# Packed 64-row TensorE products and ScalarE-issued stores in an FFT convolution gated with a GLU

## The chip, the cores and the metric

The kernel runs on one core of a Trainium2 chip. The metric is device time in microseconds (us) of one execution; lower is better. A core has five engines that each work through an instruction list of their own in order: PE (TensorE, the matmuls), DVE (VectorE), ACT (ScalarE), POOL (GpSimd) and SP (SyncE). In this kernel SP computes nothing; it issues the DMA transfers between on-chip memory (SBUF) and device memory (DRAM). Matmul results land in PSUM, in banks of 128 partitions by 512 numbers.

## What is computed

The reference mixes two branches of the same input `x` (2048 rows of 512 channels), everything in float32:

```
g   = sigmoid((x * gate_w).sum(-1, keepdims=True))
a   = S4 convolution of x:  K[d,l] = Re sum_n C[d,n] * exp(dt*A[d,n]*l) * dt*B[d,n],
      y = irfft(rfft(pad(x)) * rfft(pad(K)))[:2048] + x * Dskip
b   = (sigmoid(x @ w_gate) * (x @ w_up)) @ w_down          # inner width 1792
out = g * a + (1 - g) * b
```

## The kernel before, in words

The long convolution is done as a two-step transform of length 2048 = 32 x 64, by matmuls with constant matrices, in plain float32. The GLU branch `b` is done with matmuls on float32r parts (a high and a low part of each operand, three products per block), which is most of the matmul work.

**The stages.** All names are those of the code.

1. *Rows* (`rows`, L354 to L371): for each of 16 row blocks the first transform step of the input (matmuls at L367), stored to the DRAM tile `a_u`.
2. *K generation* (`kgen`, L191 to L241): for each of 16 channel groups of 32 channels, DVE builds powers `T` by repeated doubling (`double`, L187 to L189), PE sums them into `kst` (L220, 64 products in four 32-column tiles of the array), ACT evicts, and then comes **K's first transform step** (L227 to L236): 16 products with `kst[:, s]` (128 rows x 64) as the stationary operand and `wk[:, c]` (128 x 128, block diagonal in four 32-row blocks) as the moving operand, for the real and the imaginary part `c`, whose results stand in the upper and lower 64 partitions. The 16 products fill two PSUM banks one after the other. After every fourth group the result `kev` is stored to `a_k` (L239).
3. *Finish* (`finish`, L252 to L285): for each of 16 pairs `q` of transform rows: load constants `w_in`, `wv` and data `au`, `ak` on SP; the second transform step of input and K (`stage2`, L244 to L250: four products for `au`, four for `ak`, each of 64 output columns, two of them side by side in the array); ACT copies the input's spectrum to `uf` (L263); DVE multiplies the spectra (four at L268 and L269, then a difference and a sum at L274 and L275). Then three half-height ACT copies (L276 to L278) rearrange the product, so that each of the two rows `kb` has real and imaginary part stacked in 128 partitions, and the **inverse stage** is one 128-row product for each `kb` (L281), evicted by ACT (L283) and stored to `b_s` by SP (L284).
4. *Final*, the **last stage** (`final`, L287 to L297): for each of 16 row blocks `m`, load `b_in` from `b_s`, two 128-row products of 64 output columns with `wf` (L293), scale by `g` and add the GLU result on DVE (L296), store to `out` on SP (L297).

**GLU work in between.** `hidden` (L393; 24 matmuls at L401, then sigmoid, product and split on ACT and DVE, L408 to L411) and the down projection (L339, 9 or 12 matmuls per row block, added up at L345) come from a generator `glu`. `run_b(n)` lets it write n units' worth of work. The main part (L426 to L457) calls it between the groups of `kgen`, the `q` of `finish` and the blocks of `final`, with fixed numbers (`ROW, MID, END, LAST`, L44).

**What sets the order.** The layer that records the program orders each engine's instructions: earlier written ones have priority, later ones are taken where its own estimate of durations says that the engine would wait. The order is fixed when the program is built; on the chip each engine keeps to it and waits on semaphores. So a stretch of PE between two stages holds just the GLU matmuls that were placed there.

**Shared memory.** PSUM has the tags `fft` (2 banks, used by K's step, `stage2` and `final`), `kg` (1), `gu` (3, used by `hidden`) and `dn` (2). In the last part, SBUF tiles `au`, `ak` and `b_in` share the tag `big` with 3 buffers, `o` has 2. That part's pool ("end", L442) takes over memory of the pool "mid" of `kgen`, so its first loads wait until the last `kev` has been stored.

Of the kernel before, what the change touches and what calls it, by code (L numbers as in the profile page):

```python
# [29 lines left out]
P = 128  # L30
L, D, F, NS = 2048, 512, 1792, 128
# [9 lines left out]
NQ = 4  # L41
# [5 lines left out]
def constants():  # L47
    l1, k1 = np.arange(32)[:, None], np.arange(32)[None, :]
    ph = 2 * np.pi * l1 * (k1 + 0.25) / 32
    co, si = np.cos(ph), np.sin(ph)  # L50
    fwd = np.stack([co, -si])
    wu = np.zeros((2, 2, 32, 2, 2, 2, 32))
    wk = np.zeros((4, 32, 2, 4, 32))
    wf = np.zeros((2, 2, 32, 2, 32))
    for j in range(2):
        for c in range(2):
            for jp in range(2):
                wu[jp, j, :, jp, c, j, :] = fwd[c]
            wf[j, c, :, j, :] = fwd[c].T / L
    for j in range(4):  # L60
        for c in range(2):
            wk[j, :, c, j, :] = fwd[c]
# [10 lines left out]
    wv = wv.reshape(16, 2, P, P).transpose(0, 2, 1, 3)  # L73
    e2 = 2.0 ** np.array(KS)
    f = lambda x, *s: np.ascontiguousarray(x.astype(np.float32).reshape(s))
    return {
        "c_wu": f(wu, P, 2, P), "c_wf": f(wf, P, 64), "c_wk": f(wk, P, 2, P),
        "c_pw": f(np.stack([e2, e2 / (2 * np.pi) * np.where(np.array(KS) < 6, -1, 1)]), 1, 2 * NB),
        "c_w2": f(w2, 16, P, 2 * P), "c_wv": f(wv, 16, P, 2 * P),
    }  # L80


def body(ctx, tc, xp, xt, prm, ldt, dsk, gw, wgu, wdn, c_wu, c_wf, c_wk, c_w2, c_wv, c_pw, out):
# [7 lines left out]
    b_s = dr.tile([P, 32, D], F32, name="b_s")  # L91
# [13 lines left out]
    wk = cst.tile([P, 2, P], F32, name="wk")  # L105
# [85 lines left out]
    def kgen(pp):  # L191
        nxt = bases(pp, 0)
        for gi in range(NG):
# [30 lines left out]

            nc.vector.tensor_tensor(kst[:, :, 0], kst[:, :, 0], dskt[:, gi], op=OP.add)

            kv = [k[:, :, 32 * s4:32 * s4 + 32].rearrange("p k (j s) -> p s j k", j=4) for k in kev]  # L227
            for s in range(0, 8, 4):
                p = fps()
                for i in range(4):  # L230
                    for c in range(2):
                        mm(p[64 * c:64 * c + 64, P * i:P * i + P], kst[:, s + i], wk[:, c], start=True, stop=True,  # L232
                           tile_position=(0, 64 * c), skip_group_check=True)
                p4 = p.rearrange("p (s j k) -> p s j k", s=4, j=4)
                for i in range(2):
                    nc.scalar.activation(kv[i][:, s:s + 4], p4[:, :, :, 16 * i:16 * i + 16], AF.Copy)  # L236
            if s4 == NG // NQ - 1:
                for i in range(2):
                    nc.sync.dma_start(a_k[h, :, 16 * i:16 * i + 16], kev[i])  # L239
# [12 lines left out]
    def finish(pp):  # L252
        for q in range(16):
            w = pp.tile([P, 2, P], F32, name="w_in", bufs=2)
            nc.sync.dma_start(w, c_w2[q].rearrange("p (a b) -> p a b", a=2))
            wv = pp.tile([P, 2, P], F32, name="wv", bufs=2)
            nc.sync.dma_start(wv, c_wv[q].rearrange("p (a b) -> p a b", a=2))
            au = pp.tile([P, 2, D], F32, tag="big", bufs=3, name="au")
            nc.sync.dma_start(au, a_u[:, :, 2 * q:2 * q + 2].rearrange("c l k d -> (c l) k d"))
            ak = pp.tile([P, NQ, 2, P], F32, tag="big", bufs=3, name="ak")  # L260
            nc.sync.dma_start(ak, a_k[:, :, 2 * q:2 * q + 2].rearrange("h r k d -> r h k d"))
            uf = pp.tile([P, 2, D], F32, name="uf", bufs=2)
            stage2(lambda kb: au[:, kb], w, lambda c, p: nc.scalar.activation(uf[:, c], p, AF.Copy))  # L263
            t1 = pp.tile([P, 2, D], F32, tag="t", bufs=2, name="t1")
            t2 = pp.tile([P, 2, D], F32, tag="t", bufs=2, name="t2f")

            def mul(c, p):
                nc.vector.tensor_tensor(t1[:, c], p, uf[:, c], op=OP.mult)  # L268
# [5 lines left out]
            nc.vector.tensor_tensor(y[:, 0], t1[:, 0], t1[:, 1], op=OP.subtract)  # L274
            nc.vector.tensor_tensor(t2[:, 0], t2[:, 0], t2[:, 1], op=OP.add)  # L275
            nc.scalar.activation(y[:64, 1], y[64:, 0], AF.Copy)  # L276
            nc.scalar.activation(y[64:, 1], t2[64:, 0], AF.Copy)
            nc.scalar.activation(y[64:, 0], t2[:64, 0], AF.Copy)  # L278
            for kb in range(2):
                p = ps.tile([P, D], F32, tag="kg", name="ips")  # L280
                mm(p, wv[:, kb], y[:, kb], start=True, stop=True)  # L281
                ev = pp.tile([P, D], F32, name="evb", bufs=3)
                nc.scalar.activation(ev, p, AF.Copy)  # L283
                nc.sync.dma_start(b_s[:, 2 * q + kb], ev)  # L284
            yield  # L285

    def final(pp, wf, m):  # L287

        b = pp.tile([P, 2, D], F32, tag="big", bufs=3, name="b_in")
        nc.sync.dma_start(b, b_s[8 * m:8 * m + 8].rearrange("(j r) k d -> (r k) j d", j=2))  # L290
        p = fps()
        for j in range(2):
            mm(p[64 * j:64 * j + 64], wf, b[:, j], start=True, stop=True, tile_position=(0, 64 * j),  # L293
               skip_group_check=True)
        o = pp.tile([P, D], F32, tag="o", bufs=2, name="o")
        nc.vector.scalar_tensor_tensor(o, p, g[:, m:m + 1], accs[m], op0=OP.mult, op1=OP.add)  # L296
        nc.sync.dma_start(out[m], o)  # L297


    W = {}  # L300
# [139 lines left out]
        for v in it:  # L440
            run_b(v * MID)
    with pool("end") as pp:  # L442
        wf = pp.tile([P, 64], F32, name="wf")
        nc.sync.dma_start(wf, c_wf)
        left = UNITS - state[1]
        for n, _ in enumerate(finish(pp)):
# [58 lines left out]
```

## Time and profile before

| | |
|---|---|
| median of 3 runs | 753.5 us (752.37 to 756.16) |
| profiled execution | 753.36 us, its span 751.6 us |
| PE busy | 706.8 us (94%) |
| DVE busy | 604.9 us (80%) |
| ACT busy | 375.5 us (50%) |
| last K group's first transform step on PE (L232) | 549.2 us from the span's start |
| finish, on PE (first L248 to last L281) | 565.2 to 701.9 us |
| final, interleaved with GLU | 701.9 to 734.2 us |
| tail, final alone | 734.2 to 751.6 us |

The span is what the profiler saw of the program; the 1.76 us between it and the time lie outside. In rows of the profile, "PE L248 MATMUL x8" counts records; each plain float32 matmul leaves two records, each float32r matmul one. A busy PE is not a PE at full rate, since records overlap. A row of the chain of waits gives start, length and what was being done. In a table of windows each engine has its busy time and its instruction count, then come the granted PE clock, the DMA engines' share and GB/s.

### The profile page before, as it was taken

To read this page: it belongs to the slowest core of one execution; us is meant where nothing else is said; L and a number is where in the kernel's file an instruction comes from. 1 tells how busy PE (TensorE), PEld (TensorE's weight loads), DVE (VectorE), ACT (ScalarE), POOL (GpSimd) and SP (SyncE) were. 2 spreads that over 40 slices of the span, in tenths; PEclk is the share of its full clock that TensorE was granted. 3 is DMA by queue.
4 is the path that set the end of the run, shared out by engine and by line. 5 is a ranking of instruction groups with operands and counts; after the bars stand their busy time and mean duration, and the time that the engine had idled before them with its cause. 6 is when DMAs were issued, how large, how long until landed. Compare 5 with 4: busy or idle time off the path is not lost.

```text
span 751.6 us, 12658 instructions
## 1 busy us (share of the span) xinstructions
PE 706.8 (94%) x5024; PEld 475.2 (63%) x5024; DVE 604.9 (80%) x835; ACT 375.5 (50%) x611; POOL 3.7 (0%) x36
## 2 busy tenths in 40 slices
PE   4988889998999999999999999999999999999995
PEld 3445348877888778877787787887883323333651
DVE  5888989999999999899999898999944544454343
ACT  5364645763638274655565654546134555555200
POOL 0000000000000000000000000000000000000000
PEclk9789879999999999999999999999999999999999
DMA  6768662433025033565013350531158877774587
GB/s 221 213 204 229 170 178 97 156 104 148 32 88 183 22 115 130 194 237 175 26 57 126 100 189 8 168 115 56 57 187 284 258 241 243 225 223 147 174 285 254
DMA packets 61019, 118.64 MB, mean 158 GB/s; under 512 B 8224, under 2 KB 22944, under 8 KB 59936
## 3 DMA queue, kind: packets, MB, share of 16 engines
q1 hardware_dynamic: 60960, 117.84, 48.3%
q8 instruction: 39, 0.64, 0.3%
q14 instruction: 20, 0.16, 0.1%
HBM read 75.35 MB, written 42.47 MB: 157 GB/s over the span
## 4 chain that ended last, share of the span: by engine, by line
PE 53%; DVE 28%; ACT 8%; DMA 7%; issue 3%; SPq 0%; DVEq 0%; ACTq 0%
PE gups L401 19%; PE dps L339 12%; PE fps L248 9%; DVE T L189 6%; DVE T L188 6%; DVE tmp L187 6%; PE ips L281 4%; PE fps L367 3%; DVE h L409 2%; PE kps L220 2%; DVE hl L411 2%; DMA xs<-xt 2%; PE fps L232 2%; DMA wst<-wgu 1%; PE fps L293 1%
## 5 line engine op out<-in xcount | busy, mean ns | idle before, releaser
L401 PE MATMUL gups<-xh,gu 128*128 128x512 f32 x896 | 293.9, 402 | 15.2 <-ACT gu L381 12.5
L401 PEld LDWEIGHTS gups<-xh,gu 128*128 128x128 f32 x896 | 170.0, 191 | 71.4 <-issue 16.2
L401 PE MATMUL gups<-xl,gu 128*128 128x512 f32 x448 | 179.2, 400 | 0.0
L339 PE MATMUL dps<-dnw,hh 128*128 128x512 f32 x448 | 150.2, 402 | 3.6 <-ACT hh L410 3.0
L187 DVE TENSOR_TENSOR tmp<-T,bz 128x64 f32<-128x64 f32 (+2 forms) x96 | 114.8, 1195 | 2.3 <-issue 0.2
L189 DVE TENSOR_TENSOR T<-T,tmp 128x64 f32<-128x64 f32 (+2 forms) x96 | 114.6, 1194 | 0.7
L188 DVE TENSOR_TENSOR T<-T,bz 128x64 f32<-128x64 f32 (+2 forms) x96 | 114.6, 1193 | 0.0
L339 PEld LDWEIGHTS dps<-dnw,hh 128*128 128x128 f32 x448 | 83.5, 189 | 37.5 <-issue 11.6
L401 PEld LDWEIGHTS gups<-xl,gu 128*128 128x128 f32 x448 | 85.6, 191 | 27.4 <-issue 10.3
L339 PE MATMUL dps<-dnw,hl 128*128 128x512 f32 x224 | 89.6, 401 | 3.0 <-DVE hl L411 1.7
L408 ACT ACTIVATE sg<-gups 128x512 f32<-128x512 f32 x56 | 33.5, 598 | 70.3 <-PE gups L401 69.6
L268 DVE TENSOR_TENSOR t<-fps,uf 128x512 f32<-128x512 f32 x32 | 22.0, 688 | 57.6 <-PE fps L248 47.6
L410 ACT ACTIVATE hh<-h 128x512 fp32r<-128x512 f32 x56 | 35.1, 628 | 47.9 <-DVE h L409 47.9
L409 DVE TENSOR_TENSOR h<-gups,sg 128x512 f32<-128x512 f32 x56 | 38.1, 684 | 20.4 <-PE gups L401 20.1
L339 PEld LDWEIGHTS dps<-dnw,hl 128*128 128x128 f32 x224 | 42.3, 189 | 16.5 <-DVE hl L411 3.7
L411 DVE TENSOR_TENSOR hl<-h,hh 128x512 fp32r<-128x512 f32 x56 | 38.3, 686 | 8.9 <-ACT hh L410 8.4
L381 ACT ACTIVATE gu<-wst 128x1024 fp32r<-128x1024 f32 x28 | 29.6, 1057 | 29.4 <-PE gups L401 13.8
L345 DVE SCALAR_TENSOR_TENSOR acc<-dps,omg,acc 128x512 f32<-128x512 f32 x48 | 35.5, 746 | 10.3 <-PE dps L339 10.3
L248 PE MATMUL fps<-au,w_in 128*64 128x512 f32 x128 | 42.3, 611 | 0.3 <-DVE t L268 0.3
L236 ACT ACTIVATE kev<-fps 128x256 f32<-128x256 f32 x64 | 33.8, 678 | 16.3 <-PE fps L232 15.4
L248 PE MATMUL fps<-ak,w_in 128*64 128x512 f32 x128 | 41.2, 609 | 0.0
L367 PE MATMUL fps<-u,wu 64*128 64x512 f32 x64 | 32.4, 780 | 6.6 <-DMA u<-xp 2.9
(78 smaller groups left out, 664.5 us busy)
## 6 DMA issues: line engine op xcount, KB each, us to landing
wst<-wgu SPq DMA_DIRECT2D x28, 512.0 KB, 4.5
a_u<-evu SPq DMA_DIRECT2D x32, 256.0 KB, 3.3
a_k<-kev SPq DMA_DIRECT2D x8, 1024.0 KB, 6.0
au<-a_u SPq DMA_DIRECT2D x16, 512.0 KB, 4.8
ak<-a_k SPq DMA_DIRECT2D x16, 512.0 KB, 4.2
b_s<-evb SPq DMA_DIRECT2D x32, 256.0 KB, 2.5
b_in<-b_s SPq DMA_DIRECT2D x16, 512.0 KB, 4.6
wsd<-wdn SPq DMA_DIRECT2D x28, 256.0 KB, 3.5
```

Source lines behind the costliest of these rows:

```text
L187: nc.vector.tensor_tensor(t2, src, sb, op=OP.mult)
L188: nc.vector.tensor_tensor(dst, src, br, op=OP.mult)
L189: nc.vector.tensor_tensor(dst, dst, t2[:, :, ::-1], op=OP.add)
L236: nc.scalar.activation(kv[i][:, s:s + 4], p4[:, :, :, 16 * i:16 * i + 16], AF.Copy)
L248: mm(p[64 * kb:64 * kb + 64], w[:, kb, 64 * c:64 * c + 64], a(kb), start=True, stop=True, tile_position=(0, 64 * kb), skip_group_check=True)
L339: mm(p, a[:, hs], dnw[:, b], start=(n == 0), stop=(n == last))
L345: nc.vector.scalar_tensor_tensor(accs[t], p, omg[:, t:t + 1], accs[t], op0=OP.mult, op1=OP.add)
L367: mm(ph[jp], wu[r, jp], u[r], start=True, stop=True, tile_position=(64 * jp, 0))
L401: mm(p, gu[:, a, k, dc], b[:, dc], start=(n == 0), stop=(n == 11))
L409: nc.vector.tensor_tensor(h, pp[1], sg, op=OP.mult)
L410: nc.scalar.activation(hh, h, AF.Copy)
L411: nc.vector.tensor_tensor(hl, h, hh.bitcast(F32), op=OP.subtract)
```

## The change

- K's first step: the products are cut into two halves of 64 rows (`jh`), each a 64-row, 64-column product with a 64-column moving operand, at one of four places of the array: 32 products per group in place of 16, into two PSUM banks that are filled together.
- The inverse stage: the three ACT copies go. `y[:, 0]` is the difference and `y[:, 1]` the sum; each `kb` is two 64-row products (`c` = 0 and 1) that accumulate, with the rows of `kb` at one half of the array. The two results take one bank each of the tags `kg` and `gu`. The order of the rows of `wv` and of `b_s` follows.
- The last stage works on two row blocks at a time: 8 products of 64 rows and 32 columns. Each of its two `b_in` tiles is loaded by two transfers of 64 partitions.
- `b_s` and `out` are stored by DMAs that ACT issues; before, SP issued them.
- The tag `big` has four buffers in place of three.

```
-            for s in range(0, 8, 4):
-                p = fps()
-                for i in range(4):
+            ph = [fps(), fps()]
+            for s in range(8):
+                for jh in range(2):
+                    r = slice(64 * jh, 64 * jh + 64)
                     for c in range(2):
-                        mm(p[64 * c:64 * c + 64, P * i:P * i + P], kst[:, s + i], wk[:, c], start=True, stop=True,
-                           tile_position=(0, 64 * c), skip_group_check=True)
+                        mm(ph[jh][64 * c:64 * c + 64, 64 * s:64 * s + 64], kst[r, s], wk[r, c], start=True, stop=True,
+                           tile_position=(64 * jh, 64 * c), skip_group_check=True)
...
-            au = pp.tile([P, 2, D], F32, tag="big", bufs=3, name="au")
+            au = pp.tile([P, 2, D], F32, tag="big", bufs=4, name="au")
...
-            nc.vector.tensor_tensor(t2[:, 0], t2[:, 0], t2[:, 1], op=OP.add)
-            nc.scalar.activation(y[:64, 1], y[64:, 0], AF.Copy)
-            nc.scalar.activation(y[64:, 1], t2[64:, 0], AF.Copy)
-            nc.scalar.activation(y[64:, 0], t2[:64, 0], AF.Copy)
+            nc.vector.tensor_tensor(y[:, 1], t2[:, 0], t2[:, 1], op=OP.add)
+            pi = [ps.tile([P, D], F32, tag="kg", name="ips"), ps.tile([P, D], F32, tag="gu", bufs=3, name="ips")]
+            for c in range(2):
+                for kb in range(2):
+                    r = slice(64 * kb, 64 * kb + 64)
+                    mm(pi[kb], wv[r, c], y[r, c], start=(c == 0), stop=(c == 1), tile_position=(64 * kb, 0))
             for kb in range(2):
-                p = ps.tile([P, D], F32, tag="kg", name="ips")
-                mm(p, wv[:, kb], y[:, kb], start=True, stop=True)
                 ev = pp.tile([P, D], F32, name="evb", bufs=3)
-                nc.scalar.activation(ev, p, AF.Copy)
-                nc.sync.dma_start(b_s[:, 2 * q + kb], ev)
+                nc.scalar.activation(ev, pi[kb], AF.Copy)
+                nc.scalar.dma_start(b_s[:, 2 * q + kb], ev)
...
     def final(pp, wf, m):
-        b = pp.tile([P, 2, D], F32, tag="big", bufs=3, name="b_in")
-        nc.sync.dma_start(b, b_s[8 * m:8 * m + 8].rearrange("(j r) k d -> (r k) j d", j=2))
-        p = fps()
-        for j in range(2):
-            mm(p[64 * j:64 * j + 64], wf, b[:, j], start=True, stop=True, tile_position=(0, 64 * j),
-               skip_group_check=True)
-        o = pp.tile([P, D], F32, tag="o", bufs=2, name="o")
-        nc.vector.scalar_tensor_tensor(o, p, g[:, m:m + 1], accs[m], op0=OP.mult, op1=OP.add)
-        nc.sync.dma_start(out[m], o)
+        ph = [fps(), fps()]
+        for h in range(2):
+            b = pp.tile([P, 2, D], F32, tag="big", bufs=4, name="b_in")
+            for jb in range(2):
+                l2 = 4 * (m + jb) + 2 * h
+                nc.sync.dma_start(b[64 * jb:64 * jb + 64], b_s[l2:l2 + 2].rearrange("x k c d -> (k c) x d"))
+            for x in range(2):
+                for jb in range(2):
+                    r, o = slice(64 * jb, 64 * jb + 64), 64 * h + 32 * x
+                    mm(ph[jb][o:o + 32], wf[r], b[r, x], start=True, stop=True, tile_position=(64 * jb, o),
+                       skip_group_check=True)
+        for jb in range(2):
+            o = pp.tile([P, D], F32, tag="o", bufs=2, name="o")
+            nc.vector.scalar_tensor_tensor(o, ph[jb], g[:, m + jb:m + jb + 1], accs[m + jb], op0=OP.mult, op1=OP.add)
+            nc.scalar.dma_start(out[m + jb], o)
...
-            final(pp, wf, m)
+            if m % 2:
+                final(pp, wf, m - 1)
             run_b(LAST * left)
```

The constants `wk`, `wf` and `wv` change their layout with it.

More of the change, by code (lines that the diff above doesn't have):

```diff
@@ L58, in constants @@
                 wu[jp, j, :, jp, c, j, :] = fwd[c]
[L59 to L62, printed above, removed]
+            wk[:, j, :, c, j, :] = fwd[c]
     l2, k2 = np.arange(64)[:, None], np.arange(64)[None, :]
@@ L76, in constants @@
     return {
-        "c_wu": f(wu, P, 2, P), "c_wf": f(wf, P, 64), "c_wk": f(wk, P, 2, P),
+        "c_wu": f(wu, P, 2, P), "c_wf": f(wf, P, 32), "c_wk": f(wk, P, 2, 64),
         "c_pw": f(np.stack([e2, e2 / (2 * np.pi) * np.where(np.array(KS) < 6, -1, 1)]), 1, 2 * NB),
@@ L90, in body @@
     a_k = dr.tile([NQ, P, 32, P], F32, name="a_k")
-    b_s = dr.tile([P, 32, D], F32, name="b_s")
+    b_s = dr.tile([64, 32, 2, D], F32, name="b_s")
     dts = dr.tile([16, 32], F32, name="dts")
@@ L225, in kgen @@
             nc.vector.tensor_tensor(kst[:, :, 0], kst[:, :, 0], dskt[:, gi], op=OP.add)
-            kv = [k[:, :, 32 * s4:32 * s4 + 32].rearrange("p k (j s) -> p s j k", j=4) for k in kev]
-            for s in range(0, 8, 4):
-                p = fps()
-                for i in range(4):
+            ph = [fps(), fps()]
+            for s in range(8):
+                for jh in range(2):
+                    r = slice(64 * jh, 64 * jh + 64)
                     for c in range(2):
-                        mm(p[64 * c:64 * c + 64, P * i:P * i + P], kst[:, s + i], wk[:, c], start=True, stop=True,
-                           tile_position=(0, 64 * c), skip_group_check=True)
-                p4 = p.rearrange("p (s j k) -> p s j k", s=4, j=4)
+                        mm(ph[jh][64 * c:64 * c + 64, 64 * s:64 * s + 64], kst[r, s], wk[r, c], start=True, stop=True,
+                           tile_position=(64 * jh, 64 * c), skip_group_check=True)
+            for jh in range(2):
+                p4 = ph[jh].rearrange("p (s j k) -> p s j k", s=8, j=2)
                 for i in range(2):
-                    nc.scalar.activation(kv[i][:, s:s + 4], p4[:, :, :, 16 * i:16 * i + 16], AF.Copy)
+                    kv = kev[i][:, :, 32 * s4 + 16 * jh:32 * s4 + 16 * jh + 16].rearrange("p k (j s) -> p s j k", j=2)
+                    nc.scalar.activation(kv, p4[:, :, :, 16 * i:16 * i + 16], AF.Copy)
             if s4 == NG // NQ - 1:
@@ L257, in finish @@
             nc.sync.dma_start(wv, c_wv[q].rearrange("p (a b) -> p a b", a=2))
[L258 removed]
+            au = pp.tile([P, 2, D], F32, tag="big", bufs=4, name="au")
             nc.sync.dma_start(au, a_u[:, :, 2 * q:2 * q + 2].rearrange("c l k d -> (c l) k d"))
[L260 removed]
+            ak = pp.tile([P, NQ, 2, P], F32, tag="big", bufs=4, name="ak")
             nc.sync.dma_start(ak, a_k[:, :, 2 * q:2 * q + 2].rearrange("h r k d -> r h k d"))
```

10 lines of the change are left out of this document (5 added, 5 removed).

## The prediction

> **What bounds the kernel now.** First the page's head, then a table of windows cut at the stages' borders.
>
> ```profile
> span 751.6 us, 12658 instructions
> PE 706.8 (94%) x5024; PEld 475.2 (63%) x5024; DVE 604.9 (80%) x835; ACT 375.5 (50%) x611; POOL 3.7 (0%) x36
> ```
> ```profile
> 105.60:549.20 443.60, 432.10 (x3880) 349.10 (x3881) 427.08 (x535) 243.66 (x373) 2.82 (x26) 1.00 0.34 113
> ```
> ```profile
> 565.20:701.90 136.70, 136.13 (x433) 47.32 (x433) 66.87 (x106) 71.87 (x119) 0.00 (x0) 1.00 0.69 221
> 701.90:734.20 32.30, 32.30 (x133) 18.76 (x132) 12.90 (x18) 3.69 (x6) 0.00 (x0) 1.00 0.79 265
> 734.20:751.60 17.40, 8.43 (x29) 1.90 (x28) 5.92 (x8) 0.00 (x0) 0.00 (x0) 0.90 0.72 255
> ```
>
> The columns are PE, weight loads, DVE, ACT, POOL. So there are four limits in turn. In K generation (105.6 to 549.2) PE and DVE are both nearly full; in finish and final PE alone is; in the tail the DMA engines are (0.72). What PE waits for is not the whole story, as a busy PE overlaps records; so I take rates from the chain of waits, where pieces follow each other:
>
> ```profile
> 137.92 1.92 PE kps L220 x128
> 430.61 1.90 PE fps L232 x32
> 433.17 16.80 PE gups L401 x74
> ```
> ```profile
> 590.73 1.86 PE fps L248 x6
> 599.61 0.92 PE ips L281 x2
> ```
> ```profile
> 51.06 1.13 PE L367 MATMUL fps<-u,wu 64*128 64x512 f32 x4
> ```
>
> A GLU matmul costs 16.80/74 = 0.227 us. A full-width float32 product (two records) costs 0.93, and so does a *pair* of them at two places of the array: L248 x6 is three products in 1.86, the odd one at the price of a pair. L367 are 64-row halves with a bank each: four records, two products, in 1.13 with the tail, so row halves do run side by side. By these prices and the recorded order of instructions, the finish holds 72.5 us of L248, 32 x 0.93 = 29.8 of L281 and 111 x 0.2275 = 25.3 of GLU: 127.6 of 136.7. The other 9.1 are 105 changes between kinds of product, 0.087 us each. No wait is left in it.
>
> **The change part by part.** The instruction order of the two programs shows more than the diff: GLU matmuls move. K generation up to its last first-step product holds 1606 of them before and 1576 after, the stretch from there to the first L248 holds 60 before and 2 after, finish 111 and 186, final 95 and 108.
>
> *1. K's first step.* It takes 16 x 1.90 = 30.4 us of PE now. Afterwards each group has 64 records of 64 columns at four places. The nearest row is L220, also 64 columns at four places: 1.92/128 = 0.015 us per record, so 0.96 per group, 15 us saved in all; the other bound is no gain (1.90). L220's row has row height 128, so that four quarters overlap is an extension. The 30 GLU matmuls fewer take off another 6.8 us of PE. But DVE does not get shorter (427 of 443.6 us), and what it waits for PE is small:
>
> ```profile
> DVE T L200 <- PE kps L220: 3.5, 2, 1.8
> ...
> DVE acc L345 <- PE dps L339: 1.3, 2, 1.1
> DVE h L409 <- PE gups L401: 0.8, 2, 0.6
> ```
>
> Its waits on PE (engine, operation, what it waited for, us in total) add up to 5.6 us; the others are on ACT. So the last group comes between 0 and 11 us earlier (11: most of DVE's 16.5 idle us); I take **-5**, at 544.1.
>
> *2. The stretch from K to finish.* The chain of waits, then SP's timeline and the landing time:
>
> ```profile
> 549.21 1.90 PE fps L232 x32
> 551.11 3.40 PE gups L401 x14
> 554.51 8.43 PE dps L339 x36
> 562.95 2.27 PE gups L401 x10
> 565.21 3.81 PE fps L248 x16
> ```
> ```profile
> 551.85 0.80 SPq L239 DMA_DIRECT2D a_k<-kev  x2
> 558.77 0.33 SPq L444 DMA_DIRECT2D wf<-c_wf  x1
> 560.10 0.43 SPq L259 DMA_DIRECT2D au<-a_u  x1
> ```
> ```profile
> au<-a_u SPq DMA_DIRECT2D x16, 512.0 KB, 4.8
> ```
>
> From the last L232 to the first L248 it takes 16 us: evict, store `a_k`, and only when that has landed (558.77) SP issues the first load of the new pool; `au`, issued at 560.10, lands some 4.8 later. The 60 GLU matmuls filled this (14.1 us). In the new order two are left, 0.5 us, and the next on PE is `au`. The chain stays: the step is 0.95 shorter, but both banks now fill together, so the evictions start 0.95 later relative to it. **16.0 us stay, some 14.5 of them idle**; bounds 15 and 17 (`au` may have landed a little before PE wanted it). The first L248 comes at 560.1. The work that covered this is done later: 75 more GLU matmuls in finish (17.1 us), 13 in final (3.0).
>
> After such a stop the clock is low:
>
> ```profile
> 85.00:87.70 2.70, 0.00 (x0) 0.00 (x1) 2.70 (x4) 2.17 (x5) 0.00 (x0) 0.87 0.87 233
> 87.70:89.00 1.30, 1.27 (x3) 0.54 (x3) 1.30 (x3) 1.28 (x3) 0.00 (x0) 0.50 0.37 139
> 95.00:97.00 2.00, 1.92 (x4) 0.49 (x2) 1.98 (x5) 0.65 (x2) 0.00 (x0) 0.50 0.89 231
> ```
>
> 2.7 us without a matmul, and the granted clock is 0.50 for over 9 us of broken work. The first `q` has broken work too; 5 us at half rate lose **+2.5** (0 to 5). The Trainium skill ("TensorE: Matmul & The Clock Gate", Part 1) says that one idle window of about 3.4 us halves the clock and that 3.4 us of sustained work bring it back, by which the loss would be 1.7; the trace agrees with the halving.
>
> *3. Finish.* The ACT copies L276 to L278 go. The first of three alike, of the groups by form:
>
> ```profile
> L276 ACT ACTIVATE y<-y 64x512 f32<-64x512 f32 x16 | 10.1, 628 | 11.1 <-DVE y L274 10.9
> ```
>
> That is 30 us of ACT in all, and 0 for PE's path, since PE had no wait there. The inverse keeps its PE time: two row-half pairs, 1.86 per `q` (row L367), against 2 x 0.92. L248 in the new order stands mostly as three, the four inverse products, one: 69.8 us in all by pairs. The pure sum is 69.8 + 29.8 + 186 x 0.2275 + 77 x 0.087 = 148.6. But now there are stretches without GLU, and there DVE's chain shows:
>
> ```profile
> 565.19 1.94 PE L248 MATMUL fps<-au,w_in 128*64 128x512 f32 x8
> 567.08 1.94 PE L248 MATMUL fps<-ak,w_in 128*64 128x512 f32 x8
> 568.26 0.69 DVE L268 TENSOR_TENSOR t<-fps,uf 128x512 f32<-128x512 f32 x1 [4.53 <-PE fps L248]
> 571.26 0.68 DVE L275 TENSOR_TENSOR t2f<-t2f 128x512 f32<-128x512 f32 x1
> ```
>
> From `ak`'s start 567.08 DVE runs six operations 0.60 apart; the second bank is free after the fourth, at 570.75. The third `au` product then takes 0.93, the inverse 1.86, the fourth with `ak`'s first half 0.93 and its second half 0.93, evenly followed by DVE: 7.6 us from one DVE start to the next, against 6.8 of PE work. Counting in the order: four bare `q` of 7.6 (30.4); five with 3 to 4 GLU matmuls between (1.86 + 0.9 + 1.86 + 0.7 + 0.93 + 1.86 + changes = 8.6, 43.0); five with 24 and some (5.5 + 2.8 + 1.1 + 0.9 + 0.2 + 0.9 + 1.9 + changes = 13.9, 69.5); first and last 8.4 + 7.7. **159 us** against 136.7; bounds 148.6 and 170.
>
> *Stores on ACT.* One issue takes 0.32 us on its queue:
>
> ```profile
> 576.07 0.32 SPq L284 DMA_DIRECT2D b_s<-evb  x1
> ```
> ```profile
> b_s<-evb SPq DMA_DIRECT2D x32, 256.0 KB, 2.5
> ```
>
> ACT was at 71.9 of 136.7 us and loses 30 of copies; two issues per `q` add 0.64. I take 0. Behind an issue on ACT stands the next `uf`, for which `ak`'s second pair waits; if each issue held ACT for a landing (2.5), it would be the rival below. SP's loads no longer stand behind stores, and the fourth `big` buffer lets `au` load earlier: gain 0, as PE did not wait for them.
>
> *4. Final.* Before, ten blocks of pairs by 0.93 stood between the GLU matmuls. After, the order has sixteen blocks of *two* products (one `x`, both `jb`) with GLU between each; two products use a quarter of the eight places, and each block costs 0.93: 14.9. With 108 x 0.2275 = 24.6, 33 changes (2.9) and 0.5 of wait for the first load, as both evictions now follow the inverse, **42.9** against 32.3; bounds 40 and 48.
>
> *5. Tail.* Eight row blocks are left, before seven.
>
> ```profile
> 736.07 4.04 DMA out<-o
> 747.97 0.75 DVE o L296
> ```
>
> Each pair uses both `o` buffers and both banks, so the next scaling waits for the stores: 4.04 + 0.75 = 4.8 a round, three rounds after the first, ahead of them 1.9 (products, first scaling), behind the last 3.6 (0.7 for its second scaling, 2.9 for the store, as from 748.72 to 751.6 now): **20** against 17.4 (17 to 25). The Trainium skill ("DMA: Bandwidth & Descriptors", Rules for kernel authors) says that two transfers to disjoint partition halves serialize and are better made as one, which speaks against the halved `b_in` loads: with a row of this profile for a 64-partition transfer,
>
> ```profile
> a_u<-evu SPq DMA_DIRECT2D x32, 256.0 KB, 3.3
> ...
> b_in<-b_s SPq DMA_DIRECT2D x16, 512.0 KB, 4.6
> ```
>
> two would be 6.6 in place of 4.6, and the tail some 4 us longer; that lies in the range.
>
> **Sum:** 544.1 + 16.0 + 2.5 + 159 + 42.9 + 20 = 784.5, plus 1.8 outside the span (753.36 - 751.6) = **786 us**. The profiled execution's 753.36 stands at the median, 753.5.
>
> **The rivals.**
> - *A. Waits hidden:* finish runs at its PE sum, 148.6. For it: before it did just that. Against: the bare `q`. 786 - 10 = 776.
> - *B. ACT as the new bound:* each `q` loses 1 us as an issue holds up `uf` or an eviction; 16 us more, 802. For it: half of ACT's instructions in finish stand behind one; against: SP's issues took 0.32.
> - *C. The packing doesn't happen:* row halves run in turn. 29.8 more in finish and 14.9 in final, 831. L367's row speaks against it.
> - *D. PE work alone decides* (faster): the last group and the loads come as early as PE gets rid of work, 88 x 0.2275 + 15 = 35 us before 565.2. Then 530.2 + 148.6 + 42.9 + 20 + 1.8 = 743.5. It decides if DVE needs under 410 us in K generation; the 427 busy us speak against it, and so does the store and load chain, which no matmul shortens.
>
> **Chances.** Forecast 0.62, A 0.17, B 0.13, C 0.03, D 0.05. Bounds together: 538 + 15 + 148.6 + 40 + 17 + 1.8 = 760 and 549 + 17 + 5 + 170 + 48 + 25 + 1.8 = 816; with two in ten left out, **763 to 805**. A measurement tells 0.5% (3.8 us) from no change; faster by more than that 0.05 (D), within it 0.02, slower 0.93.
>
> **What would show it.** In the new trace: PE idle some 14 us just ahead of the first L248, with its clock low after; K's step under 1.1 us a group, but the last group less than 11 us earlier; in finish, PE waiting for DVE ahead of the third `au` product in bare `q`; in final, 16 separate pairs. I am wrong if K generation ends over 15 us earlier, if the gap is filled, or if ACT's DMA issues are seen as what PE waits for.

## The result and the profile after

The changed kernel takes 806.1 us (median of 4 runs, 804.02 to 808.65) against 754.0 (4 runs, 752.37 to 756.16) for the kernel before on the same chip: a ratio of 1.069 (95% interval 1.064 to 1.074), slower. The profiled execution took 808.65 us, its span is 806.9. The prediction was 786.0 (763 to 805).

The page's head of the changed kernel, to be set beside the first fence of the prediction:

```profile
span 806.9 us, 13923 instructions
PE 726.5 (90%) x5664; PEld 469.1 (58%) x5664; DVE 604.4 (75%) x835; ACT 346.7 (43%) x566; POOL 3.7 (0%) x36
```

DVE has the same work (604.4 against 604.9), ACT less by the copies, and PE is 80 us idle where it was 45. The stages, in windows cut at their borders; the columns are those of the prediction's windows, so the last three are granted PE clock, DMA share and GB/s:

```profile
105.60:555.50 449.90, 423.39 (x4396) 338.21 (x4387) 427.34 (x542) 245.34 (x378) 3.04 (x28) 0.99 0.35 112
555.50:570.64 15.14, 1.79 (x68) 1.32 (x67) 0.00 (x0) 1.95 (x4) 0.00 (x0) 0.72 0.63 224
570.64:738.00 167.36, 157.87 (x570) 62.33 (x570) 71.73 (x114) 43.63 (x75) 0.00 (x0) 0.98 0.58 184
738.00:786.00 48.00, 47.03 (x194) 22.04 (x192) 13.82 (x19) 4.88 (x8) 0.00 (x0) 0.98 0.70 182
786.00:806.90 20.90, 14.87 (x44) 1.90 (x44) 5.26 (x7) 0.00 (x0) 0.00 (x0) 0.53 0.70 209
```

The second row is the stretch from K to finish: PE is busy 1.79 of 15.14 us and DVE not at all. Finish (third row) went from 136.7 to 167.4 us, and PE is 9.5 us idle in it, where it was 0.6. The tail runs at a clock of 0.53.

How the stretch begins, in the chain of waits:

```profile
549.99 3.64 PE kps L217 x128
553.64 1.90 PE dps L344 x4
555.53 1.10 PE fps L229 x64
...
558.63 5.94 DMA a_k<-kev
...
565.98 4.52 DMA au<-a_u
...
570.64 1.09 PE fps L247
```

K's step for one group is 1.10 us where it was 1.90: the four 64-row quarters do run side by side. But store and load follow as before, and 570.64 - 555.53 = 15.1 us pass. The 64 products into `kst` just ahead took 3.64, before 1.92: PE had run out of GLU work already while DVE finished the last group, and its clock was at half.

A bare `q` (no GLU matmul in it), from one third `au` product to the next, in the same view:

```profile
642.49 1.04 PE fps L247 x2
643.53 1.97 PE ips L279 x8
645.50 0.59 ACT evb L282
...
646.10 0.53 ACTq L283
...
646.73 0.60 ACT evb L282
647.33 0.50 ACT uf L262
...
647.87 1.10 PE fps L247 x4
...
649.00 0.69 DVE t L267
649.69 0.61 DVE t2f L268
...
650.43 1.04 PE fps L247 x2
```

That is 7.94 us, in which PE waits for `uf` from ACT and for the second bank from DVE (L268). ACT is late with `uf` because its list has the issue of a store (ACTq L283, 0.53 us) between the two evictions of the inverse. PE's waits in finish name `uf` five times (line, what it waited for, us in total, times, longest):

```profile
PE fps L247 <- ACT uf L262: 3.4, 5, 1.1
```

Four of the five are in the bare `q`, some 0.56 us each; the fifth is told in the part on the prediction. The inverse's four packed products take 1.97, so they too run two by two.

Final, with one pair of products between GLU matmuls, sixteen times, and then the tail:

```profile
747.55 0.89 PE gups L406 x3
748.44 0.98 PE fps L297 x4
...
782.70 3.48 DMA out<-o
...
786.20 3.48 DMA b_in<-b_s
...
789.72 1.94 PE fps L297 x4
...
791.69 0.76 DVE o L301
...
792.47 4.91 DMA out<-o
...
797.40 3.83 DMA b_in<-b_s
```

In the tail a load of `b_in` starts only when a store of `out` has landed, and that twice in a row. SP's waits there name it:

```profile
SPq L293 <- DMA out<-o: 21.2, 6, 4.0
```

### The profile page after: what moved, and what is told of

Read it like the earlier page. It is cut to its first block, busy times and chain, and to the rows that moved or that the text cites. A ratio compares the mean times of both kernels' runs of the same rounds, so it can differ in the third digit from the quotient of the medians.

```text
span 806.9 us, 13923 instructions
## 1 busy us (share of the span) xinstructions
PE 726.5 (90%) x5664; PEld 469.1 (58%) x5664; DVE 604.4 (75%) x835; ACT 346.7 (43%) x566; POOL 3.7 (0%) x36
## 4 chain that ended last, share of the span: by engine, by line
DVE 35%; PE 29%; ACT 11%; DMA 6%; issue 6%; ACTq 0%; SPq 0%; DVEq 0%
PE gups L406 9%; DVE tmp L184 8%; DVE T L185 8%; PE fps L247 8%; DVE T L186 8%; PE dps L344 5%; PE ips L279 4%; PE fps L297 2%; DVE h L414 2%; DVE hl L416 2%; PE kps L217 2%; ACT L413 2%; DVE acc L350 2%; ACT L164 1%; DMA xs<-xt 1%
## 5 line engine op out<-in xcount | busy, mean ns | idle before, releaser
L406 PEld LDWEIGHTS gups<-xh,gu 128*128 128x128 f32 x896 | 170.6, 191 | 72.4 <-issue 15.1
L344 PE MATMUL dps<-dnw,hh 128*128 128x512 f32 x448 | 155.3, 410 | 11.1 <-ACT hh L415 10.4
L406 PEld LDWEIGHTS gups<-xl,gu 128*128 128x128 f32 x448 | 85.8, 192 | 21.8 <-issue 2.4
L344 PE MATMUL dps<-dnw,hl 128*128 128x512 f32 x224 | 91.6, 409 | 0.8 <-DVE hl L416 0.8
L267 DVE TENSOR_TENSOR t<-fps,uf 128x512 f32<-128x512 f32 x32 | 22.1, 689 | 70.0 <-ACT evb L282 35.1
L247 PE MATMUL fps<-au,w_in 128*64 128x512 f32 x128 | 51.6, 639 | 17.4 <-DMA au<-a_u 13.3
L247 PE MATMUL fps<-ak,w_in 128*64 128x512 f32 x128 | 47.1, 624 | 3.4 <-ACT uf L262 3.4
L262 ACT ACTIVATE uf<-fps 128x512 f32<-128x512 f32 x32 | 19.0, 595 | 67.2 <-PE fps L247 53.0
L282 ACT ACTIVATE evb<-ips 128x512 f32<-128x512 f32 x32 | 19.1, 597 | 60.5 <-PE ips L279 50.5
L217 PE MATMUL kps<-T 128*32 128x64 f32 x2048 | 35.3, 232 | 7.5 <-DVE T L186 7.5
L386 ACT ACTIVATE gu<-wst 128x1024 fp32r<-128x1024 f32 x28 | 29.6, 1057 | 28.8 <-PE gups L406 20.7
```

The lines of the kernel that those rows point to most:

```text
L217: mm(p[32 * j:32 * j + 32, s].rearrange("p (a b) -> p a b", a=2), T[:, 0, ch, c], T[:, 1:3, ch, c], start=(c == 0), stop=(c == 1), tile_po ...
L247: mm(p[64 * kb:64 * kb + 64], w[:, kb, 64 * c:64 * c + 64], a(kb), start=True, stop=True, tile_position=(0, 64 * kb), skip_group_check=True)
L344: mm(p, a[:, hs], dnw[:, b], start=(n == 0), stop=(n == last))
L406: mm(p, gu[:, a, k, dc], b[:, dc], start=(n == 0), stop=(n == 11))
```

## The experiments

Two things were in doubt. What emptied the stretch: the theory was that the inverse's second result takes a bank of the tag `gu`, which `hidden` needs for GLU work; the rival, that the new inverse or the stores on ACT are slower by themselves. And what broke up the last stage: the halved loads, or the packing. Of the recorded order one can count GLU matmuls in the stretch, in finish and in final, and the blocks in which the last stage's products stand. With the times of the stages in each profile (us; "first K" is the start of the first product of K's step, behind a start-up whose code no edit but the tenth changes):

| kernel | GLU in stretch / finish / final | blocks | first K | K's step ends | first product of finish | finish | final | tail |
|---|---|---|---|---|---|---|---|---|
| before | 60 / 111 / 95 | 9 | 105.6 | 550.8 | 565.2 | 136.6 | 32.1 | 17.7 |
| after | 2 / 186 / 108 | 17 | 109.4 | 556.4 | 570.6 | 167.1 | 44.9 | 24.3 |
| 1 inverse alone | 2 / 186 / 108 | 8 | 102.7 | 547.6 | 561.6 | 162.4 | 35.7 | 20.4 |
| 2 without the inverse | 61 / 125 / 89 | 13 | 110.5 | 556.4 | 571.2 | 139.6 | 34.6 | 29.2 |
| 3 second bank from `dn` | 61 / 169 / 45 | 4 | 108.1 | 553.3 | 567.8 | 152.0 | 14.4 | 44.3 |
| 4 one load | 2 / 186 / 108 | 5 | 106.0 | 552.6 | 567.0 | 166.4 | 31.9 | 21.8 |
| 5 K's step alone | 61 / 120 / 94 | 9 | 104.4 | 549.4 | 564.5 | 139.2 | 31.8 | 19.4 |
| 6 last stage alone | 60 / 115 / 91 | 12 | 105.5 | 550.6 | 565.0 | 137.2 | 34.0 | 53.1 |
| 7 last stage, one load | 60 / 115 / 91 | 5 | 110.4 | 554.8 | 569.4 | 137.2 | 28.5 | 19.7 |
| 8 without inverse, one load | 61 / 125 / 89 | 5 | 104.0 | 549.0 | 564.0 | 139.5 | 28.5 | 21.5 |
| 9 stores on ACT alone | 60 / 123 / 83 | 9 | 109.9 | 555.9 | 570.2 | 138.8 | 30.9 | 19.5 |
| 10 banks from `kg`, one load | 61 / 131 / 103 | 5 | 112.4 | 554.9 | 570.4 | 142.2 | 31.4 | 22.1 |
| 11 stretch filled | 59 / 138 / 78 | 12 | 106.6 | 551.8 | 566.9 | 155.4 | 31.6 | 31.6 |
| 12 experiment 7, `out` on ACT | 60 / 115 / 91 | 5 | 105.6 | 550.7 | 565.0 | 137.6 | 28.8 | 21.6 |

The column "first K" differs by 8 us between kernels that share that code (102.7 to 110.5), so a single profile tells a stage's length better than its place. From there to the end of K's step it is 442.5 to 447.0 in all. The scatter goes with the granted clock: ahead of that first product the clock stood at 0.50 for 23.9 us in experiment 1, which starts earliest, for 34.1 in the kernel before and for 51.2 in experiment 2. Over all kernels but the tenth the two rise together; which causes which is not shown.

**1. The inverse alone.** The kernel before with the new inverse, `b_s` still stored by SP.

```
+            pi = [ps.tile([P, D], F32, tag="kg", name="ips"), ps.tile([P, D], F32, tag="gu", bufs=3, name="ips")]
...
+                nc.sync.dma_start(b_s[:, 2 * q + kb], ev)
```

> The kernel before, with the inverse stage of the change alone (no copies, 64-row products, second result in a bank of the tag gu; stores still on SP, b_in as before). Theory G: the bank that the inverse now shares with hidden keeps the GLU matmuls of the finish from being placed ahead of it, so the stretch between K and finish stands empty and the finish has bare q: 14.5 us idle, 2.5 us of low clock, 10 to 14 us of waits in finish, so 780 us (775 to 786). Rival R: the emptied stretch comes from the K step or from the sum of the parts, and the inverse alone, which takes 30 us off ACT, is worth nothing or a little: 748 to 757 us.

Measured: 784.4 us, ratio 1.037 (1.030 to 1.044). This part alone empties the stretch and lengthens finish by 26 us. Its stretch and finish, in windows:

```profile
547.60:561.60 14.00, 0.99 (x10) 0.42 (x6) 0.00 (x0) 1.47 (x4) 0.00 (x0) 0.63 0.73 253
561.60:724.00 162.40, 157.88 (x570) 61.28 (x570) 71.29 (x114) 42.39 (x75) 0.00 (x0) 0.99 0.58 189
```

Finish has the 186 GLU matmuls of the changed kernel, and SP issues the stores. A bare `q`, again from one third `au` product to the next, in the chain of waits:

```profile
653.00 1.00 PE fps L248 x2
...
655.92 1.88 PE fps L248 x6
...
660.50 1.04 PE fps L248 x2
```

That is 7.50 us against 7.94, and none of PE's waits in this finish names ACT. The three bare `q` that both kernels share take 1.3 us longer in all with the stores on ACT.

**2. All but the inverse.** The changed kernel with the old inverse; stores on ACT and halved loads stay.

```
-            pi = [ps.tile([P, D], F32, tag="kg", name="ips"), ps.tile([P, D], F32, tag="gu", bufs=3, name="ips")]
+            nc.scalar.activation(y[:64, 1], y[64:, 0], AF.Copy)
...
+                p = ps.tile([P, D], F32, tag="kg", name="ips")
+                mm(p, wv[:, kb], y[:, kb], start=True, stop=True)
```

> The changed kernel with the inverse stage of before (three copies, 128-row products in kg; stores on ACT). Theory G: the stretch between K and finish is filled again, and what is left of the loss is final's separate pairs (10 us) and the tail (8 us): 772 us (767 to 780). Rival R: the loss stays, 795 us or more.

Measured: 769.8 us, 1.019 (1.012 to 1.025). The stretch is full again and finish is back; what is left over lies in final and tail. Stretch, finish and tail:

```profile
556.50:571.20 14.70, 14.45 (x66) 11.22 (x61) 4.47 (x7) 3.91 (x7) 0.00 (x0) 1.00 0.70 248
571.20:710.80 139.60, 139.56 (x446) 50.39 (x446) 67.25 (x107) 71.53 (x119) 0.00 (x0) 1.00 0.68 217
745.40:774.60 29.20, 21.35 (x82) 2.93 (x80) 8.26 (x11) 0.00 (x0) 0.00 (x0) 0.66 0.78 225
```

**3. The second result bank from another tag.** The changed kernel; only the tag of one PSUM tile is another.

```
-ps.tile([P, D], F32, tag="gu", bufs=3, name="ips")
+ps.tile([P, D], F32, tag="dn", bufs=2, name="ips")
```

> The changed kernel with one word changed: the inverse's second result takes a bank of the tag dn in place of gu. The order then has 61 GLU matmuls in the stretch, 169 in finish and only 45 in final, so nearly all of final stands in the tail. Theory G: K to finish 15 us without idle PE, finish 152 us, final 10, tail some 45 us at the rate of the changed kernel's tail, 775 us (768 to 785). Rival R (the bank has nothing to do with it, the new products are slow by themselves): 800 us or more.

Measured: 776.7 us, 1.026 (1.020 to 1.031). One word puts 59 GLU matmuls back into the stretch, and finish has no idle PE any more:

```profile
553.40:567.80 14.40, 14.17 (x66) 11.38 (x61) 3.46 (x5) 5.26 (x10) 0.00 (x0) 1.00 0.74 260
567.80:719.80 152.00, 151.67 (x553) 57.73 (x553) 69.96 (x111) 41.41 (x72) 0.00 (x0) 1.00 0.63 200
```

So it is not the inverse's products that empty the stretch but that one of their banks comes from the tag of `hidden`. The loss that is left, some 20 us, lies behind: so much GLU work now stands in finish that 58 of the 64 last-stage products come behind the last GLU matmul, and the tail is 44.3 us.

**4. One load for each tile.** The changed kernel; each `b_in` tile is one transfer of 128 partitions (the columns of `wv` are put in an order that makes its rows evenly spaced).

```
-            for jb in range(2):
-                l2 = 4 * (m + jb) + 2 * h
-                nc.sync.dma_start(b[64 * jb:64 * jb + 64], b_s[l2:l2 + 2].rearrange("x k c d -> (k c) x d"))
+            l2 = 4 * m + 4 * h
+            nc.sync.dma_start(b, b_s[l2:l2 + 4].rearrange("(x j) k c d -> (j k c) x d", j=2))
```

> The changed kernel with each b_in tile loaded by one transfer of 128 partitions in place of two of 64 (the columns of the constant wv are reordered so that the rows lie right; same work). The order then has final's 8 products of a pair of row blocks side by side: 4 blocks ahead of the last GLU matmul in place of 16. Theory L (the halved loads cost both the separate pairs and the tail): final 42.5 to about 30 us, tail 26 to about 19, so 787 us (782 to 792). Rival: the loads cost what their bytes cost, and a block is hidden by waits anyway: 803 us or more.

Measured: 788.3 us, 1.043 (1.036 to 1.049). Final goes from 44.9 to 31.9 us with the same 108 GLU matmuls: the last stage stands in 5 blocks in place of 17. SP's wait for stores ahead of a load is gone as well:

```profile
SPq L293 <- DMA out<-o: 0.4, 1, 0.4
```

**5. K's step alone.** The kernel before with the 64-row products in K's first step.

```
+            ph = [fps(), fps()]
+            for s in range(8):
+                for jh in range(2):
```

> The kernel before with K's first step packed and nothing else changed; the order keeps 61 GLU matmuls in the stretch. Theory V (DVE sets K generation): from the first to the last K group 445 us as before (444.9 to 447.0 in all runs so far, with either form of the step), no gain in time: 0 to +4 us against before. Rival P (PE sets it): 15 us of PE fewer show as 7 to 15 us less.

Measured: 757.3 us (10 runs), 1.004 (1.001 to 1.008). K generation in one window:

```profile
104.40:549.40 445.00, 424.04 (x4413) 339.58 (x4413) 426.51 (x535) 245.51 (x376) 2.85 (x26) 1.00 0.34 112
```

The kernel before has 443.6 us with 432.1 of PE and 427.1 of DVE. PE lost 8 us of work and the stage none of its length: PE does not set it, and its saved time is idle time. What is left as the bound is DVE with its 427 us of work. From the first K product to the end of DVE's last doubling it is 439.9 us in the kernel before and 437.9 to 440.6 in all fourteen kernels; no run makes DVE's work shorter, so this is argued and not tested. The order puts 9 more GLU matmuls into finish (2.0 us), which is most of the 3 us that this kernel is slower.

**6. The last stage alone.** The kernel before with the new last stage, halved loads and four `big` buffers; `out` is stored by SP.

```
-            nc.scalar.dma_start(out[m + jb], o)
+            nc.sync.dma_start(out[m + jb], o)
```

(shown against the changed kernel's `final`)

> The kernel before with the last stage of the change (pairs of row blocks, 64-row products, two half loads per tile, four big buffers), stores of b_s and out still on SP. Theory L (half loads make separate pairs and a long tail, whoever issues the stores): 21 of 32 pairs of products stand in the tail, tail 26 to 29 us against 17.7, 764 us (760 to 769). Rival A (ACT's issues make the tail long): tail 18 to 20 us, 754 to 758.

Measured: 790.5 us, 1.045 (1.040 to 1.051), 26 us above what was expected. The tail is 53.1 us. SP's waits, and then the chain:

```profile
SPq L302 <- DVE o L301: 51.9, 12, 6.8
```
```profile
748.20 5.12 DMA b_in<-b_s
...
753.37 3.13 PE fps L297 x8
756.52 0.76 DVE o L301
757.30 0.42 SPq L302
...
757.81 5.13 DMA b_in<-b_s
```

In SP's list a store of `out` (L302) stands between loads. It waits for DVE's `o`, which waits for the products, which wait for the load before; the next load is behind it on SP. So every round pays a whole load, 9.6 us. With ACT issuing the stores (experiment 2) the tail was 29.2: the stores on ACT, which cost nothing in the kernel before (experiment 9), are what keeps its halved loads from costing 24 us more.

**7. The last stage with one load.** As experiment 6 with the load of experiment 4.

> As e6, but one load of 128 partitions per tile. The order has five blocks in final, four of 8 products side by side ahead of the last GLU matmul. Theory L: final 32 to 27 us, tail 20 to 22 us against 17.7, so the packing gains about what the tail loses: 752 us (747 to 757). Rival: the tail stays at 26 us or more, 758 to 762.

Measured: 752.2 us (10 runs), 0.995 (0.992 to 0.999): a little faster than before. Final is 28.5 us, before 32.1.

**8. Without the inverse, one load.** The edits of experiments 2 and 4 together.

> The changed kernel with the inverse stage of before and one load per tile: both named causes undone, the packed K step, the packed last stage, ACT's stores and four buffers kept. Theories G and L together: 29 us of e2's tail become about 21, and nothing of the loss but a few us is left: 758 us (753 to 764). Rival: ACT's stores or the K step still cost, 768 us or more.

Measured: 753.9 us (10 runs), 1.000 (0.996 to 1.004). The whole loss is gone, with packed K step, packed last stage, stores on ACT and four buffers in place. So the loss had two places, and the rest of the change is worth nothing that can be measured.

**9. Stores on ACT alone.** The kernel before with the issuing engine changed in two lines.

```
-                nc.sync.dma_start(b_s[:, 2 * q + kb], ev)
+                nc.scalar.dma_start(b_s[:, 2 * q + kb], ev)
...
-        nc.sync.dma_start(out[m], o)
+        nc.scalar.dma_start(out[m], o)
```

> The kernel before with one edit: ScalarE in place of SP issues the stores of b_s and of the output. Theory A0 (an issue on ScalarE costs PE nothing, as in the prediction's sum): 752 to 758 us, finish and final together within 2 us of the 168.7 of before. Rival B (an issue holds up the next uf or eviction by about 1 us per q): 766 to 774 us, with PE waiting for ScalarE's uf in finish.

Measured: 755.1 us (10 runs), 0.998 (0.995 to 1.001); finish and final are 169.7 us together, before 168.7. These are all of PE's waits in them:

```profile
PE fps L293 <- DMA b_in<-b_s: 0.8, 2, 0.5
PE fps L248 <- DMA ak<-a_k: 0.5, 1, 0.5
```

No wait for ACT, so here rival B of the prediction falls. But finish is full of GLU work in this kernel. In the bare `q` of the changed kernel PE does wait behind ACT's issue (the result section and experiment 1), so "an issue costs PE nothing" holds only where other work covers it.

**10. The new inverse with banks of its own.** The changed kernel with one load, and both result banks from the tag `kg`, which gets a second bank at the expense of `gu`.

```
-            pi = [ps.tile([P, D], F32, tag="kg", name="ips"), ps.tile([P, D], F32, tag="gu", bufs=3, name="ips")]
+            pi = [ps.tile([P, D], F32, tag="kg", bufs=2, name="ips") for _ in range(2)]
...
-            p = ps.tile([P, 512], F32, tag="gu", bufs=3, name="gups")
+            p = ps.tile([P, 512], F32, tag="gu", bufs=2, name="gups")
```

> The changed kernel with two edits: both result banks of the inverse come from the tag kg, which gets two buffers while the tag of hidden keeps two of its three, and b_in is loaded by one transfer. By the instruction order 61 GLU matmuls stand between K's last step and the first product of finish again, 131 in finish, 103 in final, with the last stage in 5 blocks. Theory Q (the new inverse cost only what its second bank took from the order): first product of finish at 565 (+-4), finish 152 of the third experiment less 38 GLU matmuls of 0.2275 = 143.4, final 31, tail 21, 762 us (757 to 768). Rival S (the new inverse is slower by itself, about 1 us per q also beside GLU work): 775 us or more. Rival T (the new inverse saves PE's path 30 us of ScalarE copies): below 748 us.

Measured: 768.4 us, 1.017 (1.013 to 1.020), just above the upper end of the expected range. Finish (142.2, expected 143.4), final (31.4, 31) and tail (22.1, 21) came as worked out, and finish is full:

```profile
570.40:712.60 142.20, 142.20 (x515) 51.18 (x515) 68.12 (x108) 40.13 (x70) 0.00 (x0) 1.00 0.67 212
```

The 5 us too many are in the first product of finish, 570.4 for 565. The first K product was at 112.4, the latest of all. More than the scatter seems to be in it: the start-up had 38.9 us of half clock, and the profiles next to that (34.1 and 41.0) start at 106.6 and 108.1. The profiled execution (767.9) also lies at the median, where the other five profiles that start K after 108 lie 2.5 to 6.6 above theirs. The bank that `hidden` lost is the likely cause; no run tests it alone. Against experiment 8, 20 more GLU matmuls stand in finish and final (4.6 us of the 14.5 between the medians; against each one's own kernel before it is 13). The packed inverse does not beat the old one in any kernel here.

**11. The stretch filled by the order of writing.** The changed kernel; 60 GLU matmuls are written ahead of finish's pool.

```
+    run_b(60)
     with pool("end") as pp:
```

> The changed kernel with one edit: 60 GLU matmuls are written ahead of the pool of finish, so that 59 stand between K's last step and the first product of finish, as before; banks, inverse, loads and last stage stay those of the changed kernel. Theory Q (the emptied stretch costs its 14 us of idle PE and the half clock behind it, whatever empties it): 806.1 - 59 x 0.2275 = 13.4 - 2.5 to 4 of half clock = 789 us (784 to 794), of which up to 2 may be given back as 48 GLU matmuls fewer stand in finish. Rival (the stretch is hidden anyway, finish and final set the time): 802 to 808 us.

Measured: 786.8 us, 1.041 (1.036 to 1.045), 19.3 below the changed kernel, as expected. Stretch and finish:

```profile
552.50:566.90 14.40, 13.40 (x60) 10.43 (x59) 4.91 (x7) 3.60 (x7) 0.00 (x0) 1.00 0.72 259
566.90:722.20 155.30, 143.61 (x522) 53.48 (x522) 67.61 (x108) 40.93 (x71) 0.00 (x0) 0.99 0.61 195
```

The bank is still that of `hidden`, and finish keeps 11.7 us of idle PE with 138 GLU matmuls (waits for ACT's `uf` are 4.7 us of it), where experiment 10 has none with 131 and takes 13 us less (its other edit, one load, leaves finish as it is: experiment 4). So the shared bank costs twice: the empty stretch, and GLU work that comes in lumps of 24 with bare `q` between.

**12. Experiment 7 with `out` stored by ACT.**

> The kernel before with the new last stage, one load per tile, four load buffers (the seventh experiment) and the output stored by ScalarE. Theory L (with one load per tile SP's list has no load held up by a store, so who issues the store no longer matters): within 2 us of the seventh experiment's 752.2, and 0.992 to 1.000 of the kernel before; tail 18 to 21.5 us. Rival M (stores on SP still delay loads, as with the halved loads): 4 us or more faster than the seventh experiment, tail 15 to 16 us.

Measured: 754.1 us (12 runs), 0.999 (0.996 to 1.002). Within 2 us of experiment 7: with one load per tile no difference by who issues the store can be measured. The tail of 21.6 is at the upper end of the 18 to 21.5 expected. Experiment 7 has the lowest ratio of all, 0.1 to 0.8% below the kernel before; its interval and that of experiment 12 overlap.

## Why the prediction was wrong in size and right in kind

Slower, the empty stretch, the low clock, the bare `q` and the sixteen separate pairs came as predicted; the time came 20 us above. Three terms failed: the 5 us credited to K's first step, of which nothing came; the stores on ACT, put at nothing, behind whose issue PE waits in every bare `q`; and the tail, which lacked a load in each round. By the sum's own terms, with the profiled execution:

| step | predicted | measured | off by |
|---|---|---|---|
| last group's K step starts | 544.1 | 555.5 | +11.4 |
| stretch | 16.0 | 15.1 | -0.9 |
| low clock and finish | 2.5 + 159 | 167.1 | +5.6 |
| final | 42.9 | 44.9 | +2.0 |
| tail | 20 | 24.3 | +4.3 |

The five add up to 22.4, which takes the predicted end of the span, 784.5, to the 806.9 measured. The profiled execution lies 2.5 above the median, and its late start (below) is of about that size.

- **Part 1, K's first step, failed.** "Between 0 and 11 us earlier" with -5 taken: the bound of no gain was right, and experiment 5 shows it: nothing from 8 us less of PE work. The prediction had read DVE's row itself ("DVE does not get shorter") and credited 5 us all the same, from waits on PE that add up to 5.6. They did not shrink: from 105.6 to 549 us they are 6.7 (5.6 before), and from 110 to 540 they are 5.0 (5.6 before), nearly all of that in one row of DVE's waits (3.5 before):

```profile
DVE T L197 <- PE kps L217: 4.8, 4, 1.7
```

3.8 us more are the late first K product (109.4 for 105.6), inside the 8 us by which that start varies with no edit to it. Of the other 2.6, 1.7 are the half clock ahead of the stretch, at L217's 3.64 us; the prediction had a low clock only behind it.
- **Part 2, the stretch, held.** 15.1 us with 1.8 of PE work. What the prediction did not name is the cause. It took the moved GLU matmuls from the recorded order; experiments 3 and 11 show that a PSUM tag shared with `hidden` moved them, and what it costs in finish besides.
- **Part 3, finish, had the right mechanism for the bare `q`, and missed ACT in it.** Experiment 1, with the stores on SP, has a finish of 162.4 us and bare `q` of 7.5: the predicted 161.5 and 7.6 nearly to the point, by DVE's chain alone. In the changed kernel a bare `q` takes 7.9, one with 3 to 4 GLU matmuls in each of two places 8.7 to 8.9 (8.6 predicted), one with 24 of them 14.3 to 14.5 (13.9). The ends of the inverse show four, six and five of them beside the first; the last `q` was taken for 7.7 and is of the second kind. Once a conversion of down-projection weights stood in ACT's list between the two evictions of a `q` and waited for its load, and PE waited 1.12 us behind it, the longest of its waits for `uf`. In ACT's timeline:

```profile
638.10 0.63 ACT L387 ACTIVATE dnw<-wsd 128x512 fp32r<-128x512 f32 x1 [1.42 <-DMA wsd<-wdn]
```

The chain of waits goes back from there through a load of weights for 4.70 us and so overstates it; most of that time PE was at work, and this `q` took 9.5 us. The first `q` began at half clock, which lasted 5.1 us (570.6 to 575.8; 3.3 us in experiment 1), so some 2.6 us of work were lost where 2.5 were taken: 11.1 us to the end of its inverse, 8.4 + 2.5 predicted. Of the 4.7 us that this finish is longer than that of experiment 1, 0.9 are in the first `q` and 1.3 in the shared bare ones. The rest is in `q` whose GLU work the two orders place otherwise, the wait behind the conversion included.
- **Stores on ACT at 0 failed in the bare `q`.** The term holds where GLU work fills finish (experiment 9). In the four bare `q` of the changed kernel the issue stands ahead of `uf`, as the prediction's own sign of being wrong has it, and costs PE a wait of 0.56 us and the `q` 0.4. That is the mechanism of rival B, at about half its price and in four `q` of sixteen. For the last stage with halved loads the stores on ACT are worth much: without them SP's list costs 24 us (experiments 6 and 2).
- **Part 4, final, held.** Sixteen pairs at 0.98. That halved loads go with the separate pairs was not seen; experiment 4 shows it, 13 us.
- **Part 5, the tail, was too short by 4 us.** The working had `o`'s buffers as the limit, a store and a scaling a round. In the chain a round also has a load in it, as SP issues a load of `b_in` only when a store has landed: 3.83 + 1.94 + 0.76 + 4.91 and some 0.1 of gaps are 11.5 us. The half clock has a part in it: the pair of products takes 1.94 there and 0.98 in final, twice in the chain. One load per tile takes that wait away (experiment 4: 21.8). The estimate by "DMA: Bandwidth & Descriptors" of the Trainium skill (Rules for kernel authors: transfers to disjoint partition halves serialize and are better made as one), a tail 4 us longer, has the size that came; as the chain is made up otherwise, that does not test it. The advice holds here by the 18 us of experiment 4, but most of that comes through the order of the products; no run times two halves against a whole by themselves.
- **Rivals.** A (waits hidden) fell with 9.5 us of idle PE in finish. B came close in time (802) by luck: its mechanism is there, but it makes some 2 us and not 16. C fell with the 1.97 us of the inverse's four products. D fell with experiment 5: less PE work does not end K generation sooner. (The "ten blocks" of the kernel before in part 4 are nine pairs in eight blocks ahead of the tail; the sum does not use them.)

What stays open: why the clock and the start-up scatter, why a load of `b_in` waits for a store of `out` to land, and by which rule the recording layer moves GLU work when a bank is shared or a load is halved. The moves were seen in the order and in the times, not in the layer itself.

## What to carry to other kernels

Before packing matmuls, ask which engine sets that stage: PE time saved beside a full DVE comes back as idle PE. A new buffer from a pool that background work uses takes that work out of the stretches that it was to fill, so count the filler in the recorded order at every edit, and give the new result its own bank or write the filler ahead of the wait. A transfer cut in two doubles the places where it can stand behind something else in an in-order list. And a test of one part in the old kernel tells its price there: the stores on ACT were free in a full finish and not in the empty places that another part of the change had made.

## What the hardware showed unexpectedly

- Quarters of the array with 64 rows and 64 columns work at once: 64 records of such products in 1.10 us, against 32 full-height ones in 1.90.
- The half clock can last through long broken work: 20.9 us of tail at 0.53, in the changed kernel, and the last 45 us of experiment 6 at 0.50 throughout. It need not: the tail of the kernel before, with PE busy 8.43 of 17.40 us, ran at 0.90. What decides it, these runs don't show.

```profile
744.00:789.40 45.40, 28.39 (x72) 3.25 (x68) 7.51 (x10) 0.00 (x0) 0.00 (x0) 0.50 0.52 145
```

- There PE is "busy" 28 of 45 us, and in the changed kernel four records of the last stage take 1.94 us in the tail, 0.98 in final. A busy share at half clock says little.
